# Filter loads that no longer wait for one another: the 32-byte cells shared by neighbouring rows are tracked for one of the two rows

## The chip, the cores and the metric

The kernel runs on 1 core of one Trainium2 chip. The metric is the device time of one execution in microseconds (us). Times carry some noise: seven to eleven runs of the kernel before, on one chip, spread over 2 to 4%. Times are therefore compared as ratios within one call on one chip, and mechanisms are read from the profiled executions, whose spans are about 1.8 us shorter than their times. A run counts as slow when it is over 1.5% above the fastest of the same kernel in its call; ratios use the fast runs alone.

## The reference, cut to what matters

The program is one block of a network: a spectral mixer followed by a token MLP, both with a layer norm before them.

```python
def _A_ref(x, w_r, w_i):                      # x: 1 x 2048 x 512
    X = rfft2(x)                              # -> 2048 x 257 complex
    X = X * (w_r + 1j * w_i)                  # the filter: two 2048 x 257 bf16 arrays
    return irfft2(X)
# h  = x + A(layernorm(x))
# h2 = h + MLP(layernorm(h))                  # w1: 2048 x 1376, w2: 1376 x 2048
```

## The kernel before

The transforms are matmuls with constant matrices. In order: F1 and F2 (forward; F2's result is copied to CS), X (its result is multiplied by the filter on VectorE, giving V), G1, G2, G3 (inverse), H (add the input), a layer norm HH, the first MLP matmul with W1, a gelu, the second with W2.

The filter sits on chip as `Wr` and `Wi`, 32 rows of 257 bf16 elements in each partition:

```python
add("Wr", [NP, NG, 257], bf, rw)              # a row is 514 bytes
add("Wi", [NP, NG, 257], bf, rw + 16448)
```

A small builder records every operation with what it reads and writes, derives the waits, orders the operations by a list scheduler, and emits one stream per engine. Memory is tracked in cells of 32 bytes:

```python
CELL = 32
def cells(self, ap):                          # the 32-byte cells that an access touches
    ...
    c = np.unique(np.concatenate([b // CELL, (b + esz - 1) // CELL]))
    quads = range(p0 // 32, (p0 + pn - 1) // 32 + 1)
    return [q * 16384 + int(x) for q in quads for x in c]
...
for ap in outs:
    for c in self.cells(ap):
        w = self.writer.get(c)
        if w is not None and w is not o:
            deps[id(w)] = w                   # a write waits for the cell's last writer
```

Since 514 is no multiple of 32, the end of a row and the start of the next share a cell. (Not at row 16: 16 x 514 = 8224 = 257 x 32.) Loads of neighbouring rows thus look like two writes to the same place, although no byte is written twice. The loads of the filter:

```python
for g0, g1 in ((0, 8), (8, 16), (16, 32)):
    n = (g1 - g0) * 257
    for w, dram in ((0, A_w_r), (1, A_w_i)):
        d = Wx[w][0:64, g0:g1, :]
        dma(f"ld_w{w}p_{g0}", d, ..., outs=[d], prio=28)
        h0 = g0
        if g0 == 0:
            for comp in range(2):
                d = Wx[w][64 + comp * 32:96 + comp * 32, 0:1, :]
                dma(f"ld_w{w}z{comp}", d, ..., outs=[d], prio=28)
            h0 = 1
        for comp in range(2):
            d = Wx[w][64 + comp * 32:96 + comp * 32, h0:g1, :]
            dma(f"ld_w{w}m{comp}_{g0}", d, ..., outs=[d], prio=28)
dma("ld_IF", IF[:], ..., prio=27)             # 1 MB
for q in range(4):
    dma(f"ld_w1_{q}", W1[:, sl, :], ..., prio=26)     # 4 x 1.4 MB
dma("ld_b1a", ...); dma("ld_b1b", ...); dma("ld_b2", ...)   # prio=25
```

Ten of the 22 filter loads carry a wait for another one: rows 1 to 7 of the upper partitions (m, four loads) for row 0 (z); rows 8 to 15 (p, two loads, and m, four) for rows 0 to 7. All DMAs go through SyncE's one in-order queue. The scheduler takes the operation that can start first, and looks at the priority only among equals:

```python
st = max(eng_free[e], dep_ready, avail, o.not_before)
key = (st, -o.prio, o.idx)
```

The reader is VectorE, two multiplies (`Wr`, `Wi`) for each of eight groups of four rows:

```python
K.op(f"x_{u}_w{w}", "dve", tt, ins=[Wx[w][:, 4 * u:4 * u + 4, 1:257]], outs=[V[:, w, 4 * u:4 * u + 4, :]], ..., prio=11)
```

## Time and profile before

| | before |
|---|---|
| time, median of 3 runs | 173.71 us |
| span of the profiled run (whose time was 171.13) | 169.3 us |
| TensorE busy | 130.2 us (77%) |
| first V starts, last V ends | 49.11, 70.03 us |
| first H starts | 74.80 us |
| from first H to the end | 94.5 us |

The profile's page first. It cuts the span into 40 slices of 4.2 us; each digit is the busy share of a slice in tenths, and for PEclk the clock that TensorE was granted. The last line is the chain of waits that ended last, by engine.

```profile
span 169.3 us, 2071 instructions
...
PE   0057859940006986599999999999999999999980
...
PEclk9999987995555599959999999999999999999998
...
PE 56%; SPq 26%; DVE 9%; DMA 3%; ACT 2%; issue 1%; DVEq 0%
```

TensorE is empty for three slices (38 to 51 us), and its clock is at half for five slices from there (0.5 means half clock). The chain leads through SyncE's queue (SPq) for 26% of the span: the program waits for DMAs to be issued. The timeline of SyncE shows which. Columns: start, duration of the issue (not of the transfer), engine, line, what was loaded, how many. A load has landed when all its bytes have arrived and its semaphore says so.

```profile
4.15 2.08 SPq L516 DMA_DIRECT2D Wr<-in_A_w_r_dram  x3
6.27 1.75 SPq L516 DMA_DIRECT2D Wi<-in_A_w_i_dram  x3
8.07 1.70 SPq L516 DMA_DIRECT2D Wr<-in_A_w_r_dram  x3
9.81 5.03 SPq L516 DMA_DIRECT2D Wi<-in_A_w_i_dram  x3
14.87 4.70 SPq L516 DMA_DIRECT2D IF<-c_IF  x1
19.62 2.03 SPq L516 DMA_DIRECT2D W_77<-in_B_w_dram  x4
21.69 0.47 SPq L515 DMA_DIRECT2D B1s<-in_B_b_dram  x1
22.21 18.70 SPq L516 DMA_DIRECT2D B2s<-in_B_b_dram  x1
40.95 1.66 SPq L516 DMA_DIRECT2D Wr<-in_A_w_r_dram  x3
42.66 3.31 SPq L516 DMA_DIRECT2D Wi<-in_A_w_i_dram  x3
...
48.56 0.81 SPq L516 DMA_DIRECT2D Wr<-in_A_w_r_dram  x2
50.08 1.12 SPq L516 DMA_DIRECT2D Wi<-in_A_w_i_dram  x2
```

The first twelve filter loads are those without a wait: rows 0 to 7 in part, and rows 16 to 31. Then come IF and the four loads of W1 (named W_77 here), and then the issue of B2s, 4 KB, which takes 18.70 us. Nothing in the program makes B2s wait for a semaphore. The Trainium skill (Perfetto Trace Analysis, "DMA Instruction — HWDGE (DVE, Sync)") says that the reported window of such an instruction starts once its semaphores are satisfied; this trace agrees: the load at 48.56 us waits for one that landed at 48.54, and only 0.31 us are reported for it (0.81 for the two in that line). So the 18.70 us are no wait for a semaphore. They end 0.3 us after the third of the four W1 loads landed (40.65 us): the issue seems to be held until the queue ahead of it has drained so far. What limits the queue is not shown. Only at 40.95 us come the loads of rows 1 to 7, with the first of rows 8 to 15. The landings that these six wait for had come at 15.3 to 17.2 us, over 20 us before.

The timeline of VectorE shows who waits for them (in brackets: idle time before the instruction, and what ended it):

```profile
47.05 0.17 DVE L728 CAST B2f<-B2s 128x16 f32<-128x16 bf16 x1 [26.62 <-DMA B2s<-in_B_b_dram]
49.11 1.22 DVE L666 TENSOR_TENSOR V<-ps,Wr 128x1024 bf16<-128x1024 f32 x1 [1.88 <-DMA Wr<-in_A_w_r_dram]
...
68.81 1.23 DVE L666 TENSOR_TENSOR V<-ps,Wi 128x1024 bf16<-128x1024 f32 x1
...
74.80 0.69 DVE L716 TENSOR_TENSOR H<-ps,X 128x512 bf16<-128x512 f32 x1 [4.51 <-PE ps L521]
```

VectorE sits idle from about 20 us to 47, and the first V starts when `Wr` lands. One window of the table by windows (columns: stretch, length, then busy us and count of PE, PEld, DVE, ACT, POOL, then PEclk, DMA share, GB/s):

```profile
40.00:44.00 4.00, 0.00 (x0) 0.00 (x0) 0.00 (x0) 0.00 (x0) 0.00 (x0) 0.50 1.03 248
```

No engine works; the DMA engines are full, but mostly with the wrong bytes. Counted from the trace's packets, 0.46 of the 1.03 are pieces of W1, which has its first reader at about 80 us, and 0.18 are packets of 2 and 32 bytes, those of the biases B1s and B2s. The filter rows have 0.38, and start at about 42 us only.

### The profile page before, as it was taken

Reading aid. Unit: us, or ns where it says so; the run is one execution under the profiler, and the core shown is the slowest. Engines: PE = TensorE matmul, PEld = TensorE weight load, DVE = VectorE, ACT = ScalarE, POOL = GpSimd, SP = SyncE. Lnnn points to the kernel's source line nnn. Section 1 sums busy time; section 2 is a strip of 40 time slices with the busy share of each in tenths; the row PEclk is TensorE's granted clock in tenths of the full one; section 3 lists DMA queues with packets and bytes.
Section 4 is the critical chain, followed back from the end, with each engine's and each line's share of the span. In section 5 each row is a group of like instructions: output and inputs, shape, how many; then the busy total and the mean of one; then the engine's idle time right before and its main releaser. Section 6 shows DMA issues by size and latency. Waiting matters only on the chain.

```text
span 169.3 us, 2071 instructions
## 1 busy us (share of the span) xinstructions
PE 130.2 (77%) x784; PEld 78.1 (46%) x784; DVE 87.8 (52%) x199; ACT 71.9 (42%) x128; POOL 7.8 (5%) x14
## 2 busy tenths in 40 slices
PE   0057859940006986599999999999999999999980
PEld 0044534720004653467665544444455666666650
DVE  1977500000037999538999995797445333223320
ACT  3178976970002245548996555975341000000000
POOL 0054600000000000000000000000000000000000
PEclk9999987995555599959999999999999999999998
DMA  5999999999963599870000000000000211110110
GB/s 167 350 372 218 183 165 363 417 429 360 157 142 64 167 340 304 261 269 0 0 0 0 4 0 0 0 2 0 4 0 0 77 47 62 64 64 31 62 62 33
DMA packets 11978, 22.18 MB, mean 131 GB/s; under 512 B 2528, under 2 KB 8672, under 8 KB 11200
## 3 DMA queue, kind: packets, MB, share of 16 engines
q1 hardware_dynamic: 11968, 22.05, 43.7%
q8 instruction: 6, 0.10, 0.2%
q14 instruction: 4, 0.03, 0.1%
HBM read 19.95 MB, written 2.10 MB: 130 GB/s over the span
## 4 chain that ended last, share of the span: by engine, by line
PE 56%; SPq 26%; DVE 9%; DMA 3%; ACT 2%; issue 1%; DVEq 0%
PE ps L521 56%; SPq L516 25%; DVE V L666 8%; DMA Wi<-in_A_w_i_dram 3%; ACT PQ L527 1%; DVE OUT L756 0%; ACT U_58 L740 0%; ACT SG_61 L746 0%; SPq L515 0%; DVE P_60 L745 0%; DVE GT L748 0%; DVE Q_59 L742 0%; DVE Q_59 L743 0%; DVEq L421 0%
## 5 line engine op out<-in xcount | busy, mean ns | idle before, releaser
L521 PE MATMUL ps<-HH,W_77 128*128 128x512 bf16 (+1 forms) x176 | 40.5, 379 | 0.0
L521 PE MATMUL ps<-EM,V 128*128 128x128 bf16 x128 | 12.1, 243 | 18.9 <-DVE V L666 18.2
L521 PEld LDWEIGHTS ps<-HH,W_77 128*128 128x128 bf16 (+1 forms) x176 | 17.4, 100 | 18.0 <-ACT HH L594 0.5
L756 DVE SCALAR_TENSOR_TENSOR OUT<-ps,B2f,H 128x512 bf16<-128x512 f32 x16 | 12.0, 751 | 24.2 <-PE ps L521 24.2
L527 ACT ACTIVATE PQ<-ps 128x512 bf16<-128x512 f32 x16 | 8.9, 595 | 26.0 <-PE ps L521 25.7
L521 PE MATMUL ps<-FS,X 128*128 128x256 bf16 x64 | 10.1, 316 | 12.5 <-POOL FS L611 11.6
L521 PEld LDWEIGHTS ps<-EM,V 128*128 128x128 bf16 x128 | 8.8, 109 | 23.0 <-issue 15.7
L728 DVE CAST B2f<-B2s 128x16 f32<-128x16 bf16 x1 | 0.2, 175 | 26.6 <-DMA B2s<-in_B_b_dram 26.6
L521 PEld LDWEIGHTS ps<-FS,X 128*128 128x128 bf16 x64 | 6.7, 113 | 15.6 <-POOL FS L611 12.4
L716 DVE TENSOR_TENSOR H<-ps,X 128x512 bf16<-128x512 f32 x16 | 10.6, 662 | 4.5 <-PE ps L521 4.5
L580 DVE BATCH_NORM_STATS2 st_93<-X 128x6 f32<-128x512 bf16 x16 | 10.4, 668 | 3.7 <-DMA X<-in_A_x_dram 3.7
L527 ACT ACTIVATE CS<-ps 128x512 bf16<-128x512 f32 x16 | 10.3, 782 | 2.3 <-PE ps L521 2.1
L580 DVE BATCH_NORM_STATS2 st_98<-H 128x6 f32<-128x512 bf16 x16 | 11.0, 690 | 0.2
L594 ACT ACTIVATE HH<-H,nb_102,rs_101 128x512 bf16<-128x512 bf16 x12 | 9.7, 810 | 3.3 <-DVE nb_102 L592 3.3
L666 DVE TENSOR_TENSOR V<-ps,Wr 128x1024 bf16<-128x1024 f32 x8 | 9.7, 1217 | 2.7 <-DMA Wr<-in_A_w_r_dram 1.9
L521 PE MATMUL ps<-EM,Y 128*128 128x256 bf16 x64 | 10.0, 303 | 1.4 <-ACT Y L527 1.4
L527 ACT ACTIVATE EO<-ps 128x512 bf16<-128x512 f32 x16 | 9.2, 588 | 3.6 <-PE ps L521 3.6
L521 PE MATMUL ps<-EM,PQ 128*128 128x256 bf16 x64 | 10.0, 295 | 0.8 <-ACT PQ L527 0.8
L666 DVE TENSOR_TENSOR V<-ps,Wi 128x1024 bf16<-128x1024 f32 x8 | 9.8, 1225 | 1.1 <-DMA Wi<-in_A_w_i_dram 0.6
L521 PE MATMUL ps<-EO,IF 128*128 128x256 bf16 (+1 forms) x48 | 10.3, 326 | 0.0
L527 ACT ACTIVATE Y<-ps 128x1024 bf16<-128x1024 f32 x8 | 7.9, 1022 | 1.8 <-PE ps L521 1.7
L521 PEld LDWEIGHTS ps<-EM,Y 128*128 128x128 bf16 x64 | 5.9, 106 | 5.1 <-ACT Y L527 1.9
(71 smaller groups left out, 181.9 us busy)
## 6 DMA issues: line engine op xcount, KB each, us to landing
W_77<-in_B_w_dram SPq DMA_DIRECT2D x4, 1376.0 KB, 18.6
out_dram<-OUT SPq DMA_DIRECT2D x16, 128.0 KB, 1.8
X<-in_A_x_dram SPq DMA_DIRECT2D x3, 512.0 KB, 7.1
Wr<-in_A_w_r_dram SPq DMA_DIRECT2D x4, 257.0 KB, 11.8
Wi<-in_A_w_i_dram SPq DMA_DIRECT2D x4, 257.0 KB, 12.5
IF<-c_IF SPq DMA_DIRECT2D x1, 1024.0 KB, 15.5
EM<-c_EM SPq DMA_DIRECT2D x1, 768.0 KB, 10.4
Wr<-in_A_w_r_dram SPq DMA_DIRECT2D x1, 514.0 KB, 11.3
```

Of the source, the lines that this page charges most:

```text
L516: return eng.dma_start(dst, src)
L521: return eng.matmul(outf(bank), lhsT, rhs, start=start, stop=stop, **({"skip_group_check": True} if skip else {}))
L527: return eng.activation(dst, srcf(bank), ACT.Copy)
L580: K.op(f"ln{which}_st{i}", "dve", lambda s, eng, bank: eng.bn_stats(st[:, i, 0:6], src), ins=[src], outs=[st[:, i, 0:6]], dur=680.0, prio= ...
L594: K.op(f"ln{which}_ap{i}", "act", lambda s, eng, bank: eng.activation(dst, src, ACT.Identity, bias=c, scale=b), ins=[src, b, c], outs=[dst ...
L666: return eng.tensor_tensor(ov, src, wv, ALU.mult)
L716: K.op(f"h_{s2}", "dve", lambda s, eng, bank, xs=xs, hs=hs: eng.tensor_tensor(hs, ps[:, bank, :], xs, ALU.add), ins=[xs], outs=[hs], dur=6 ...
L728: K.op("b2f", "dve", lambda s, eng, bank: eng.tensor_copy(B2f[:, :], B2s[:, :]), ins=[B2s[:, :]], outs=[B2f[:, :]], dur=80.0)
L756: K.op(f"fin{s2}", "dve", lambda s, eng, bank, dst=dst, bia=bia, hs=hs: eng.scalar_tensor_tensor(dst, ps[:, bank, :], bia, hs, op0=ALU.add ...
```

## The change

The intent: a shared cell needs one owner among the loads. Each load now declares its last row only up to column 239, so that the shared cell belongs to the load of the next row alone, and V's reads are declared up to column 239 likewise. Bytes, transfers and arithmetic stay as they were. The row's last 17 columns arrive with the same load as its other columns, so whoever waits for the row waits for them too. The list scheduler runs anew, though.

```diff
+    def w_cells(w, p0, p1, h0, h1):
+        res = [Wx[w][p0:p1, h1 - 1:h1, 0:240]]
+        if h1 - h0 > 1:
+            res.append(Wx[w][p0:p1, h0:h1 - 1, :])
+        return res
+
     for g0, g1 in ((0, 8), (8, 16), (16, 32)):
         ...
-            d = Wx[w][0:64, g0:g1, :]
-            dma(f"ld_w{w}p_{g0}", d, ..., outs=[d], prio=28)
+            dma(f"ld_w{w}p_{g0}", Wx[w][0:64, g0:g1, :], ..., outs=w_cells(w, 0, 64, g0, g1), prio=28)
         ...                                  (the same for the z and m loads; each z now stands before its m)
-            K.op(f"x_{u}_w{w}", "dve", tt, ins=[Wx[w][:, 4 * u:4 * u + 4, 1:257]], ...
+            K.op(f"x_{u}_w{w}", "dve", tt, ins=[Wx[w][:, 4 * u:4 * u + 4, 1:240]], ...
```

More of the change, by code (lines that the diff above doesn't have):

```diff
@@ L547, in build_kernel @@
         for w, dram in ((0, A_w_r), (1, A_w_i)):
-            d = Wx[w][0:64, g0:g1, :]
-            dma(f"ld_w{w}p_{g0}", d, bass.AP(dram.tensor, g0 * 257, [[64 * 257, 32], [0, 2], [1, n]]), 64 * n * 2, outs=[d], prio=28)
-            h0 = g0
-            if g0 == 0:
-                for comp in range(2):
-                    d = Wx[w][64 + comp * 32:96 + comp * 32, 0:1, :]
-                    dma(f"ld_w{w}z{comp}", d, bass.AP(dram.tensor, 32 * 257, [[64 * 257, 32], [1, 257]]), 32 * 514, outs=[d], prio=28)
-                h0 = 1
-            for comp in range(2):
-                d = Wx[w][64 + comp * 32:96 + comp * 32, h0:g1, :]
-                dma(f"ld_w{w}m{comp}_{g0}", d, bass.AP(dram.tensor, (64 - h0) * 257, [[64 * 257, 32], [-257, g1 - h0], [1, 257]]),
-                    32 * (g1 - h0) * 514, outs=[d], prio=28)
+            dma(f"ld_w{w}p_{g0}", Wx[w][0:64, g0:g1, :], bass.AP(dram.tensor, g0 * 257, [[64 * 257, 32], [0, 2], [1, n]]), 64 * n * 2,
+                outs=w_cells(w, 0, 64, g0, g1), prio=28)
+            h0 = max(g0, 1)
+            for comp in range(2):
+                p0, p1 = 64 + comp * 32, 96 + comp * 32
+                if g0 == 0:
+                    dma(f"ld_w{w}z{comp}", Wx[w][p0:p1, 0:1, :], bass.AP(dram.tensor, 32 * 257, [[64 * 257, 32], [1, 257]]), 32 * 514,
+                        outs=w_cells(w, p0, p1, 0, 1), prio=28)
+                dma(f"ld_w{w}m{comp}_{g0}", Wx[w][p0:p1, h0:g1, :],
+                    bass.AP(dram.tensor, (64 - h0) * 257, [[64 * 257, 32], [-257, g1 - h0], [1, 257]]),
+                    32 * (g1 - h0) * 514, outs=w_cells(w, p0, p1, h0, g1), prio=28)
     B1s, B1f, B2s, B2f = (T[n] for n in ("B1s", "B1f", "B2s", "B2f"))
@@ L666, in tt @@
                 return eng.tensor_tensor(ov, src, wv, ALU.mult)
-            K.op(f"x_{u}_w{w}", "dve", tt, ins=[Wx[w][:, 4 * u:4 * u + 4, 1:257]], outs=[V[:, w, 4 * u:4 * u + 4, :]],
+            K.op(f"x_{u}_w{w}", "dve", tt, ins=[Wx[w][:, 4 * u:4 * u + 4, 1:240]], outs=[V[:, w, 4 * u:4 * u + 4, :]],
                  dur=1230.0, unit=unit, pr=True, last=w == 1, prio=11)
```

## The prediction

> **What bounds the kernel now.** Three stages follow one another in the 169.3 us span. The chain of waits gives SyncE's issue 26%, VectorE's filter multiply V 8% and TensorE 56%. Up to 37 us TensorE does the forward transform. Then the timeline shows TensorE idle for 14.1 us, 36.4 to 50.5, until the first V; the table by windows gives granted clock 0.50 there and DMA share 1.03 at 40 to 44 us. V runs 49.11 to 70.04 (16 multiplies of 1.22 us: VectorE is the limit). From 71.83 the chain is nearly pure TensorE to the end. So the hole before V is on the critical path; its cause is when the filter rows land.
>
> The DMA issue timeline shows why they land late. The loads of rows 1 to 7, and of rows 8 to 15, wait for loads that share a 32-byte cell with them. The scheduler therefore put IF (1 MB), the four W_77 loads (5.6 MB), B1s and B2s ahead of them. The SyncE queue fills: the B2s issue alone takes 18.70 us, 22.21 to 40.91. Only at 40.95 come the six Wr/Wi loads that the first V needs, and four more at 48.56 to 50.89. The Trainium skill (DMA: Bandwidth & Descriptors, "Anatomy of one DMA") says that semaphore waits are held by the issuing sequencer, not the DMA engines; this trace agrees, in that nothing behind a held issue moves.
>
> **What changes.** No byte and no compute instruction is added or removed. Ten loads lose their wait, and with priority 28 against 27 and 26 all 22 filter loads are issued ahead of IF and W_77. B1s still has one shared-cell wait.
>
> **Costing (estimates from packet records of this trace).** The filter loads start near 11 us. 514-byte packets take about 60 ns on one of 16 engines. Rows 0 to 7 cost about 6 us, rows 8 to 15 about 6, rows 16 to 31 about 13 (12 to 25 us here, at 188 GB/s). So they land near 19, 26 and 36 us. IF and W_77 (426 GB/s here) slip by about 8 us, to 50. That is no loss: their first readers come later than that.
>
> The first V then no longer waits for DMA. Its matmuls end at 28.2 us here (the last needed CS copy and matmuls in the timeline). V takes 16 x 1.22 = 19.6 us, plus 1 to 2 us because f2 matmuls and CS copies now share TensorE and ScalarE with it: V ends near 49 to 50 instead of 70.0. V for rows 16 up is wanted near 38, just after they land. From V's end to the first H takes 4.8 us here, from first H to the end 94.5 us. Hence first H near 55 and a span near 150. One give-back: VectorE converts B2s and B1s in order before the first H, and those land only after W_77, near 54 to 55. I expect that wait to end about when H could start anyway.
>
> Adding the 2 to 3 us by which times exceed the span: **153 us**, range **149 to 160**. Faster by over 2%: 0.97; within 2%: 0.02; slower: 0.01.
>
> **What would show it.** Filter issues all before IF, none later than about 25 us; first V near 28; no 14 us idle of TensorE and no clock of 0.50 near 40 to 55 (the skill's TensorE: Matmul & The Clock Gate, Part 1, says idleness halves the clock; the 0.50 here agrees); V 20 to 22 us long; first H near 55; the last 94 us unchanged.
>
> **What would make it wrong.** B2f conversion placed inside the V chain would hold VectorE until about 55 and push the span to 156. Row 16-and-up loads slower than estimated would stall the fifth V. W2 loads ahead of the last B1s load could delay its conversion.

## The result, and the profile after

| | before | after |
|---|---|---|
| time, median | 174.61 us (4 runs) | 150.62 us (4 runs) |
| span of the profiled run | 169.3 | 147.6 |
| first V starts | 49.11 | 26.76 |
| last V ends | 70.03 | 48.22 |
| first H starts | 74.80 | 53.23 |
| from first H to the end | 94.5 | 94.3 |

The ratio of the times is 0.8727 (95% interval 0.8578 to 0.8876). A ratio is the mean time of one kernel's fast runs over that of the other's of the same rounds, so not quite the ratio of the medians quoted. Two of the four runs before (176.37 and 175.5 us) count as slow. Where too few fast runs left none, the text says that the medians are divided.

The span is 21.8 us shorter (169.34 less 147.56). By the table, 22.35 of it is the earlier first V. The V stage gives back 0.5 (21.46 us long instead of 20.92), the way from the last V to the first H 0.2; the rest gains 0.2.

The page of the changed kernel:

```profile
span 147.6 us, 2073 instructions
...
PE   0038875998994799999999999999999999999970
...
PEclk9999999999999779999999999999999999999996
...
PE 71%; ACT 10%; DVE 9%; DMA 4%; POOL 1%; issue 1%; SPq 1%; DVEq 0%
```

TensorE's hole is gone; its clock dips to 0.7 in two slices, where it was at half in six; and SyncE's queue has fallen from 26% of the chain to 1%. Its timeline:

```profile
4.16 2.97 SPq L516 DMA_DIRECT2D Wr<-in_A_w_r_dram  x5
7.17 2.59 SPq L516 DMA_DIRECT2D Wi<-in_A_w_i_dram  x5
9.80 1.79 SPq L516 DMA_DIRECT2D Wr<-in_A_w_r_dram  x3
11.63 2.66 SPq L516 DMA_DIRECT2D Wi<-in_A_w_i_dram  x3
14.33 3.17 SPq L516 DMA_DIRECT2D Wr<-in_A_w_r_dram  x3
17.54 4.95 SPq L516 DMA_DIRECT2D Wi<-in_A_w_i_dram  x3
22.53 3.59 SPq L516 DMA_DIRECT2D IF<-c_IF  x1
26.16 2.18 SPq L516 DMA_DIRECT2D W_77<-in_B_w_dram  x4
...
28.91 19.45 SPq L516 DMA_DIRECT2D B2s<-in_B_b_dram  x1
```

All 22 filter loads now precede IF. B2s is held for 19.45 us, about as long as before, but no load that anybody urgently needs stands behind it. The semaphore records of the trace give the landings: rows 0 to 7 complete at 18.5 us, rows 8 to 15 at 23.8, rows 16 to 31 at 29.7 (`Wr`) and 35.6 (`Wi`), the last of W1 at 52.0.

VectorE:

```profile
26.76 1.22 DVE L672 TENSOR_TENSOR V<-ps,Wr 128x1024 bf16<-128x1024 f32 x1 [6.66 <-PE ps L521]
...
33.46 1.23 DVE L672 TENSOR_TENSOR V<-ps,Wr 128x1024 bf16<-128x1024 f32 x1 [1.73 <-PE ps L521]
...
46.99 1.22 DVE L672 TENSOR_TENSOR V<-ps,Wi 128x1024 bf16<-128x1024 f32 x1
52.84 0.17 DVE L734 CAST B2f<-B2s 128x16 f32<-128x16 bf16 x1 [4.62 <-DMA B2s<-in_B_b_dram]
53.23 0.69 DVE L722 TENSOR_TENSOR H<-ps,X 128x512 bf16<-128x512 f32 x1 [0.21 <-PE ps L521]
```

The first V now waits for TensorE, not for a DMA. There is one hole of 1.73 us before the third group, and the cast of B2s, which stands before the first H in VectorE's order, waits 4.62 us for its DMA. It is done at 53.01 us and H's matmuls end at 53.19, so in this execution the cast holds up nothing. The window that was empty before:

```profile
40.00:44.00 4.00, 3.95 (x53) 2.61 (x53) 3.97 (x4) 2.53 (x5) 0.00 (x0) 1.00 1.02 428
```

The DMA engines are as full as before, while TensorE and VectorE are busy at full clock.

### The profile page after: what moved, and what is told of

Read it like the earlier page. It is cut to its first block, busy times and chain, and to the rows that moved or that the text cites. A ratio compares the mean times of both kernels' runs of the same rounds, so it can differ in the third digit from the quotient of the medians.

```text
span 147.6 us, 2073 instructions
## 1 busy us (share of the span) xinstructions
PE 125.3 (85%) x784; PEld 75.9 (51%) x784; DVE 87.9 (60%) x199; ACT 71.9 (49%) x128; POOL 7.7 (5%) x14
## 4 chain that ended last, share of the span: by engine, by line
PE 71%; ACT 10%; DVE 9%; DMA 4%; POOL 1%; issue 1%; SPq 1%; DVEq 0%
PE ps L521 71%; DVE V L672 7%; ACT Y L527 4%; DMA FP<-c_FP 4%; ACT CS L527 2%; POOL FS L617 1%; ACT FS L616 1%; SPq L516 1%; ACT PQ L527 1%; DVE OUT L762 1%; ACT U_58 L746 0%; ACT SG_61 L752 0%; ACT FP L605 0%; ACT sd_95 L579 0%; DVE P_60 L751 0%
## 5 line engine op out<-in xcount | busy, mean ns | idle before, releaser
L521 PE MATMUL ps<-FS,X 128*128 128x256 bf16 x64 | 10.7, 328 | 11.5 <-POOL FS L617 10.8
L527 ACT ACTIVATE CS<-ps 128x512 bf16<-128x512 f32 x16 | 11.3, 750 | 2.2 <-PE ps L521 1.9
L521 PE MATMUL ps<-EM,V 128*128 128x128 bf16 x128 | 9.8, 220 | 2.6 <-DVE V L672 2.3
L521 PE MATMUL ps<-EM,Y 128*128 128x256 bf16 x64 | 9.3, 274 | 2.1 <-ACT Y L527 1.4
L521 PEld LDWEIGHTS ps<-EM,V 128*128 128x128 bf16 x128 | 7.6, 98 | 4.9 <-DVE V L672 3.4
L521 PEld LDWEIGHTS ps<-EM,PQ 128*128 128x128 bf16 x64 | 6.7, 106 | 2.7 <-ACT PQ L527 1.0
L617 POOL TENSOR_SCALAR FS<-FP,rs_96 128x256 bf16<-128x256 bf16 x8 | 7.4, 922 | 12.8 <-ACT FP L605 7.9
(71 smaller groups left out, 171.3 us busy)
```

What stands on the lines that cost most here:

```text
L521: return eng.matmul(outf(bank), lhsT, rhs, start=start, stop=stop, **({"skip_group_check": True} if skip else {}))
L527: return eng.activation(dst, srcf(bank), ACT.Copy)
L617: return eng.tensor_scalar(FS[:, :, i, :], FP[:, :, i, :], rs, None, op0=ALU.mult)
```

## The experiments

The theory, A: what cost the time was the *place* of ten loads in the in-order queue behind 6.7 MB that nobody needs yet (IF and W1). The scheduler put them there because of the waits. Rival B: the waits themselves cost it, that is the idle time between one load's landing and the next one's start. Other rivals are named where they are tested. Twelve runs on four chips; every kernel gave the right result.

### e2_old_place: no waits, but the old place in the queue

Edit of the changed kernel:

```diff
-   outs=w_cells(w, 0, 64, g0, g1), prio=28)
+   outs=w_cells(w, 0, 64, g0, g1), prio=24 if g0 == 8 else 28)
-   outs=w_cells(w, p0, p1, h0, g1), prio=28)
+   outs=w_cells(w, p0, p1, h0, g1), prio=28 if g0 == 16 else 24 if g0 == 0 else 23)
```

> The changed kernel, no waits between filter loads, but the ten loads that used to wait are given a lower priority, so that they are issued after IF, W_77, B1s and B2s, where the kernel before had them. Theory A (place in the queue): these loads are issued from about 41 us, the first V starts near 48 to 49, the span is 166 to 169 us, the ratio to before 0.97 to 1.0. Rival B (the waits themselves): the gain stays, ratio near 0.87.

Measured: 173.06 us against 172.12, ratio 1.0059 (0.9989 to 1.0129); span 171.3. SyncE and VectorE:

```profile
44.99 0.92 SPq L516 DMA_DIRECT2D Wr<-in_A_w_r_dram  x2
```

```profile
51.73 0.17 DVE L734 CAST B2f<-B2s 128x16 f32<-128x16 bf16 x1 [30.53 <-DMA B2s<-in_B_b_dram]
52.28 1.23 DVE L672 TENSOR_TENSOR V<-ps,Wr 128x1024 bf16<-128x1024 f32 x1 [0.37 <-DMA Wr<-in_A_w_r_dram]
```

The whole gain is gone, although no filter load waits for another. The first V came later than the 48 to 49 us expected, because the issue of B2s began 1.5 us later here and was held for 21.20 us: the loads behind it were issued from 44.99 us instead of 41, and the last `Wr` rows that V needs landed at 52.2. (The cast of B2s, just before, ended at 51.91 and cost nothing.) Span and ratio lie a little above A's range as well. Without the better place, removing the waits is worth nothing.

### e1_waits_kept: the waits kept, the big loads held back

Edit of the kernel before (`nb` is the scheduler's earliest start):

```diff
+NB = 21800.0
-    dma("ld_IF", ..., prio=27)
+    dma("ld_IF", ..., prio=27, nb=NB)                (the same for ld_w1_*, ld_b1a, ld_b1b, ld_b2)
```

> The kernel before with every wait between filter loads kept, but IF, W_77, B1s and B2s held back in the list so that all 22 filter loads are issued ahead of them. Theory A (the place in SyncE's queue is what cost the time, the wait itself costs about one landing): loads of rows 0 to 7 then queue behind rows 16 to 31 and land near 31 us, rows 8 to 15 near 38; first V near 31 (26.8 in the changed kernel, 49.1 before), V ends near 53, first H near 57.5, span near 152, a ratio to before of 0.88 to 0.92. Rival B (the waits themselves, each exposed in full, cost the 22 us): first V still after 45 and the ratio above 0.96.

Measured: 158.01 us, 0.918 of 172.12 (medians; the two fast runs of the four give 0.910 of the fast runs before); span 155.1. First V at 32.55, last V's end at 55.73, first H at 60.73.

```profile
32.55 1.22 DVE L667 TENSOR_TENSOR V<-ps,Wr 128x1024 bf16<-128x1024 f32 x1 [11.13 <-DMA Wr<-in_A_w_r_dram]
```

Rival B's 0.96 is excluded, but A's figure was 3 us short in the span. Rows 0 to 7 landed at 32.5 (`Wr`) and 33.7 (`Wi`), behind rows 16 to 31, so the order among the filter loads still hurt. That left open how much of the shortfall is order and how much is waits.

### e10_waits_kept_in_order: the waits kept, the loads in the order of need

Edit of the kernel before:

```diff
+NB16 = 18100.0
+NB = 18400.0
-            dma(f"ld_w{w}p_{g0}", ..., prio=28)
+            dma(f"ld_w{w}p_{g0}", ..., prio=28, nb=NB16 if g0 == 16 else 0.0)       (the same for the m loads)
-    dma("ld_IF", ..., prio=27)
+    dma("ld_IF", ..., prio=27, nb=NB)                (the same for ld_w1_*, ld_b1a, ld_b1b, ld_b2)
```

> The kernel before with every wait between filter loads kept, but issued in the order in which V needs them: rows 0 to 7, then 8 to 15, then 16 to 31, then IF, W_77, B1s, B2s. The other engines have the order of the changed kernel. Theory A refined (what cost the time is what the scheduler put ahead of the waiting loads; a wait by itself is one landing, 2 to 3 us each for two levels): rows 0 to 7 land near 22, rows 8 to 15 near 28, all before V wants them; rows 16 to 31 near 41, about 1 us late; first V near 27 to 28.5, span 148 to 152, ratio to before 0.87 to 0.895. Rival B (the waits themselves): ratio 0.92 or more, as with the waits kept and rows 16 to 31 ahead.

Measured: 154.72 us against 173.44, ratio 0.8992 (0.8933 to 0.905); span 151.6. SyncE's own waits and VectorE's timeline:

```profile
SPq L518 <- DMA Wr<-in_A_w_r_dram: 9.2, 3, 7.6
```

```profile
26.71 1.22 DVE L668 TENSOR_TENSOR V<-ps,Wr 128x1024 bf16<-128x1024 f32 x1 [6.66 <-PE ps L523]
...
47.34 1.22 DVE L668 TENSOR_TENSOR V<-ps,Wi 128x1024 bf16<-128x1024 f32 x1
57.38 0.17 DVE L730 CAST B2f<-B2s 128x16 f32<-128x16 bf16 x1 [8.82 <-DMA B2s<-in_B_b_dram]
57.47 0.68 DVE L718 TENSOR_TENSOR H<-ps,X 128x512 bf16<-128x512 f32 x1
```

SyncE does wait, 9.2 us in three waits for `Wr`, the longest 7.6 instead of the 2 to 3 expected for one (the load waited for was in the queue behind EM, which landed at 14.13), and between 12 and 16 us the DMA share falls to 0.54 (1.12 in the changed kernel). Yet the first V starts at 26.71 and the last ends at 48.57, as in the changed kernel (26.76 and 48.22): the V stage loses nothing. The loss comes later. The DMA time lost in the waits delays everything in the queue; B2s lands at 57.36 us instead of 52.82, and its cast holds the first H until 57.47, though H's matmuls had ended at 53.35. The hold is 4.1 us, and the span exceeds the changed kernel's by 4.0. One landing alone would prove little, since B2s landed as late in one execution without waits (e4, 57.74). But the ratios say the same: 0.8992 against 0.8727 and 0.8758 is 4.0 to 4.6 us of 172. So of the gain of 21.8 us about 17.7 comes with the place in the queue (169.34 less 151.59), and about 4 with the removal of the waits, by way of the cast of B2s. A's figure (0.87 to 0.895) was missed by a little, B's "0.92 or more" by more.

One thing is not separated. When the list scheduler places the loads early, it also reorders the other engines: in the traces, VectorE and ScalarE have one order in the kernel before and in e2, and another in the changed kernel, e1 and e10. No run has the new place with the old order. The trace before bounds what the order can explain: there, in the old order, the first V's matmuls had ended at 28.2 us, and the last `Wr` load that it waited for landed at 49.03. So at least 20.8 of the 22.35 us by which the first V came earlier are the load's. What the old order would have cost after the first V is not shown.

### e3_rows01_only: four of the ten waits removed

Edit of the changed kernel, in `w_cells`: a load of several rows declares all of them in full, so that rows 8 to 15 wait for rows 0 to 7 again.

```diff
-            res.append(Wx[w][p0:p1, h0:h1 - 1, :])
+            return [Wx[w][p0:p1, h0:h1, :]]
```

> Only the waits of rows 1 to 7 on row 0 are taken away (4 of the 10 loads); the loads of rows 8 to 15 still wait for those of rows 0 to 7. Theory A with 'the last of the waits decides': V of the first two groups starts near 27 us, then the third V waits for rows 8 to 15, which land near 52; V ends near 67, span 163 to 167, ratio 0.96 to 0.985. Rival C (the gain is shared among the waits that are taken away): 4 of 10 waits give about 40 per cent of the gain, 8 to 9 us, ratio near 0.95 or under.

Measured: 171.12 us (166.95 to 174.44), 0.994 of 172.12 (medians). Only one of the four runs counts as fast, 166.95 us, 0.970 of the fast runs before and within A's range. The profiled run was the slowest of the four and counts as slow, so its times are rough. In it the first two groups of V run from 28.0 us, and VectorE then sits idle for 21 us, until the cast of B2s at 54.39, which here stands before the third group. That group then waits for rows 8 to 15, which land at 56.8 us (`Wr`) and 59.9 (`Wi`), against the 52 expected:

```profile
56.99 2.35 DVE L672 TENSOR_TENSOR V<-ps,Wr 128x1024 bf16<-128x1024 f32 x2 [2.43 <-DMA Wr<-in_A_w_r_dram]
```

Rival C (the gain in proportion to the waits removed, a ratio near 0.95 or under) is not borne out: none of the four runs reached it. How much under 1 the ratio truly is stays open between these runs. In the trace the last of the waits decides, not their number.

### e4_old_reads and e5_new_reads_only: the second hunk by itself

e4 is the changed kernel with V's reads declared up to column 256 again; e5 is the kernel before with that hunk alone.

```diff
-            ... ins=[Wx[w][:, 4 * u:4 * u + 4, 1:240]], ...      (e4; e5 is the reverse, in the kernel before)
+            ... ins=[Wx[w][:, 4 * u:4 * u + 4, 1:257]], ...
```

> The changed kernel with the second hunk undone: V's reads name columns 1 to 256 again. The list and every engine's order are the same; only the semaphores that the second V group waits for differ (it waits for rows 8 to 15 as well, which land at 23.8 us, before the second group at 29.3). Theory A: the same time, ratio to before 0.86 to 0.885, V from about 26.8. Rival F (the shortened read carries part of the gain): slower than the changed kernel by over 2 per cent.

> The kernel before with the second hunk alone: V's reads name columns 1 to 239, the loads still wait for one another. Theory A: the same as before, ratio 0.985 to 1.015, first V near 49. Rival F: faster than before by over 2 per cent.

Measured: e4 152.13 us, ratio 0.8709 (0.8642 to 0.8777); e5 172.05 us, 0.990 of 173.78 (medians), first V at 50.88. e4, with two fast runs, is as fast as the changed kernel, so the shortened read is not needed for the gain. e5 is less clear: its two fast runs give 0.982 of the fast ones before, a little under the 0.985 expected and short of rival F's 2 per cent, and TensorE has a slightly different order in it. The e4 profile shows something else. It fell in an execution with late DMAs, and there the cast of B2s did hold up the first H:

```profile
57.77 0.17 DVE L734 CAST B2f<-B2s 128x16 f32<-128x16 bf16 x1 [7.83 <-DMA B2s<-in_B_b_dram]
57.85 0.68 DVE L722 TENSOR_TENSOR H<-ps,X 128x512 bf16<-128x512 f32 x1
```

H's matmuls had ended at 54.91 us, so the hold was 2.9 us.

### e7_two_w1_first: how much slack the filter loads have now

```diff
-        dma(f"ld_w1_{q}", ..., prio=26)
+        dma(f"ld_w1_{q}", ..., prio=28.5 if q < 2 else 26)
```

> The changed kernel with two of the four W_77 loads (2.8 MB, about 6.7 us of DMA time) issued ahead of all filter loads; every other engine has the same order. Filter rows all land 6.7 us later: rows 0 to 7 at about 25 (wanted 26.8), rows 16 to 31 of Wi at about 42.2 (wanted 39.8). Theory A (only the part of a delay beyond the slack counts): span 2 to 3 us longer than the changed kernel, ratio to before about 0.885. Rival D (each us of delay of the filter loads costs a us): 6.7 us longer, ratio about 0.91.

Measured: 153.63 us, ratio 0.8827 (0.8715 to 0.8939); span 149.2. One V waits:

```profile
42.67 1.22 DVE L672 TENSOR_TENSOR V<-ps,Wi 128x1024 bf16<-128x1024 f32 x1 [3.13 <-DMA Wi<-in_A_w_i_dram]
```

Rows 16 to 31 of `Wi` landed at 42.5 us, wanted at 39.8 in the changed kernel; rows 0 to 7 landed at 25.6, still before the first V at 26.6. The delay of about 7 us costs a hole of 3.1, and the last V ends 3.0 us later (51.19). The span grows by 1.7, since part is made up before the first H (54.94 against 53.23). Rival D's 6.7 us is excluded by the profile, and its 0.91 by the interval of the ratio, which rests on two fast runs. That the delay costs anything at all, only the profile shows.

### e0, e6 and e11: does the wait for B2s cost anything?

e0 is the changed kernel again. e6, and e11 which is the same kernel, move the three bias casts behind the H stage in VectorE's order:

```diff
-    K.op("b2f", "dve", ..., dur=80.0)
+    K.op("b2f", "dve", ..., dur=80.0, not_before=60000.0)        (the same for b1f_a and b1f_b)
```

> The changed kernel once more, as the measure for the other runs of this call. Ratio to before 0.86 to 0.885; V from 26.8 to 48.2 us with one hole of 1.7 us before the third group; VectorE idle for about 4.6 us until B2s lands, then first H near 53.2.

> The changed kernel with the three casts of the bias vectors moved behind the H stage in VectorE's order, nothing else changed. Theory A (the 4.6 us that VectorE waits for B2s end as H's matmuls end, so they cost nothing): first H within 0.3 us of the changed kernel, ratio to it 0.995 to 1.005. Rival E (the wait for B2s is the next limit): first H up to 4 us earlier, ratio 0.975 to 0.985.

> The changed kernel with the bias casts behind the H stage, once more, to settle whether it beats the changed kernel. B2s landed at 52.8, 54.6 and 57.7 us in three profiled executions with the same SyncE order, and VectorE's wait for it held the first H by about 0.3, 1.6 and 3.2 us. If that is a cost of the average run: ratio to before 0.865 to 0.873, 0.5 to 1 per cent under the changed kernel (0.873 and 0.876 so far). If not: 0.873 to 0.88.

Measured: e0 151.82 us, ratio 0.8758 (0.8679 to 0.8838); e6 150.79 us, 0.8706 (0.8629 to 0.8784); e11 149.93 us, 0.8715 (0.8651 to 0.8779). In the profiles (that of e6 is slow) the hold goes away: in e0 the cast held the first H for 1.7 us (H's matmuls ended at 53.03, H started at 54.72); in e6 and e11 H follows its matmuls by 0.04 us. But in those two executions the first V was also 1.5 us later (28.53 and 28.38 us against 26.94), with EM, loaded before any filter, landing 2 us later. So the spans came out the same (149.2, 149.1, and 148.9 for e0). (By the same reading, the 0.3, 1.6 and 3.2 us in e11's expectation are 0, 1.7 and 2.9.) The ratios lie in the direction of a gain of about half a per cent, but their intervals overlap almost wholly. A version better than the changed kernel is therefore not shown.

### e8_x_first and e9_x_first_casts_late: the hole before the third group, and the cast inside the chain

e8 gives the X matmuls a higher priority than G1; e9 is e8 with the casts late as in e6.

```diff
-                       unit, cs == 0, cs == 1, first, 11, 128)
+                       unit, cs == 0, cs == 1, first, 13, 128)
```

> The changed kernel with the priority of the X matmuls raised from 11 to 13, above those of G1. The hole of 1.7 us before the third V group goes, but the list now puts the cast of B2s into the V chain, before the last V group. Theory A with in-order engines (the hazard named in the prediction): VectorE stops there until B2s lands near 52.8, V ends near 55.3, first H near 60, span 5 to 7.5 us longer than the changed kernel, ratio to it 1.035 to 1.05. If the cast's place does not matter: 1 to 2 us shorter, ratio 0.99.

> Both: X matmuls first, and the casts moved behind the H stage. Theory A: the hole of 1.7 us goes and nothing takes its place: V ends near 46.5, first H near 51.6, span 1 to 2 us shorter than the changed kernel, ratio to it 0.988 to 0.993. If it is not faster, the hole was slack or was filled by another wait of the shared TensorE and ScalarE.

Measured: e8 159.40 us, ratio 0.9253 (0.9188 to 0.9318), which against e0 is 1.056, above the 1.035 to 1.05 expected; e9 151.87 us, 0.8772 (0.8701 to 0.8843). The hole before the third group went in both. In e8 the list put the cast into the V chain (the profiled run is slow):

```profile
57.59 0.17 DVE L734 CAST B2f<-B2s 128x16 f32<-128x16 bf16 x1 [8.73 <-DMA B2s<-in_B_b_dram]
57.68 1.22 DVE L672 TENSOR_TENSOR V<-ps,Wr 128x1024 bf16<-128x1024 f32 x1
```

e8 and e9 differ in the place of the cast of B2s alone, as their traces confirm, and by 7.5 us in the median (8.3 in the mean of the fast runs): that is the hazard that the prediction named. e9 shows that the hole was not to be had for free. Its V stage is longer than the changed kernel's, 23.3 us (27.21 to 50.47) instead of 21.5:

```profile
38.53 1.23 DVE L672 TENSOR_TENSOR V<-ps,Wr 128x1024 bf16<-128x1024 f32 x1 [1.47 <-PE ps L521]
40.39 1.22 DVE L672 TENSOR_TENSOR V<-ps,Wi 128x1024 bf16<-128x1024 f32 x1 [0.64 <-DMA Wi<-in_A_w_i_dram]
```

Further holes of 0.7 us follow before the seventh and eighth groups. The expected 1 to 2 us of gain is a miss. Why the changed kernel's own hole arises was not tested.

## Why the prediction was right

- *What bounds the kernel, and why.* Right. e2 shows that the place in the queue carries most of the time: with the old place and no waits the gain is zero. e10 shows that with the waits and a good order the first V is on time. (The order of the other engines changes together with the place; see e10.)
- *All filter loads ahead of IF, the last issued by about 25 us, landing near 19, 26 and 36 us.* Issued until 22.5; landed at 18.5, 23.8 and 35.6. The packet times of the trace before were enough to place 4.2 MB of loads within 2.2 us.
- *First V near 28.* It came at 26.76. This term was over-sized by 1.4 us: 28.2 was read off the trace before, in which TensorE ran at 0.57 of its clock between 24 and 28 us; after, the table gives 1.00 for that stretch. The Trainium skill (TensorE: Matmul & The Clock Gate, Part 1) explains half clock by a lack of recent activity. The 0.50 in the long hole agrees with that; why the short dip at 24 us was absent after was not tested; TensorE's longest idle stretch just before it was 0.87 us in both traces.
- *V 20 to 22 us long, ending near 49 to 50.* 21.5 us long, ending at 48.2.
- *First H near 55, held until then by B2s.* 53.23. B2s landed at 52.8, not 54 to 55, and in the profiled run its cast ended 0.2 us before H's matmuls, so the expectation that it costs nothing held there. It does not hold in general: e0 lost 1.7 us to it, e4 2.9, e10 4.1. The two ends met by coincidence, and the coincidence changes with the execution.
- *The last 94 us unchanged.* 94.5 before, 94.3 after, and 94.1 to 94.7 in all twelve other profiles. The time of the first H settles the time of the kernel.
- *153 us.* 150.62: the first H was 1.8 us earlier than predicted, and a time exceeds its span by 1.8 us, not by 2 to 3. Both errors are sizes; no step failed.
- *SyncE holds a wait, so that nothing behind a held issue moves.* The Trainium skill (DMA: Bandwidth & Descriptors, "Anatomy of one DMA") states that the issuing sequencer holds the semaphore waits. The held issue that the prediction had in view, that of B2s, waits for no semaphore; e10 is the better evidence, and agrees. There SyncE issued nothing from 7.70 us to 15.35, when the load waited for had landed (15.34), and rows 16 to 31 landed at 39.7 us instead of 35.6.
- *What could make it wrong: the cast of B2s inside the V chain, 156 us.* It did not happen in this change. e8 brought it about, and cost 7.5 us against e9 (8.3 between the fast runs), more than the 6 predicted.

## What to carry to other kernels

Here a false dependency between DMAs on one in-order queue cost about 4 us as a wait, and about 18 by what the list scheduler put ahead of the held loads. So read the issue order first, and count the bytes in front of the load that the next stage needs. Then look for trivial instructions that wait for the last DMA of the queue (here a cast of 2048 numbers): they can bind as soon as the real work ahead of them is done early.

## What the Trainium skill lacked or had wrong

- DMA: Bandwidth & Descriptors, "Specifications", gives 512 B as the smallest transfer for line rate. The 514-byte rows here do not come near it: in the kernel before, from 22 to 24 us, when 599 of 625 packets were of 514 B (about 59 ns each on their engine), the DMA engines were full (share 1.17) and moved 166 GB/s, while the changed kernel moved 422 to 428 GB/s from 36 to 44 us, when the 11,008-byte pieces of W1 were under way. Later on the same page it is said that descriptors not starting on a 256-byte boundary cost extra beats; no run here separates that cause from the size.
- No page says how long an issue is held when the queue is full: 18.70 us before and 19.45 us after, for a 4 KB load, while the DMA engines moved 6.8 MB each time.
- No page gives the spread of landings between executions of an unchanged issue order. EM, the seventh load, with the same six loads ahead of it in every kernel here, landed between 12.5 and 18.5 us; where the first V waited for TensorE alone, it started between 26.6 and 28.8 us, later with a later EM on the whole. Fixed positions of casts in an in-order engine turn that spread into lost time.
